# Chunk attention and gated feed-forward on one core: a new order of the first loads, more transposes by DMA, and other transfer times in the planner

## The chip, the core and the metric

The kernel runs on one core of a Trainium2 chip. A core has TensorE (PE, with its weight loads PEld), VectorE (DVE), ScalarE (ACT), GpSimd (POOL), SyncE (SP), which computes nothing and issues transfers here, and 16 DMA engines. The metric is the device time of one execution in microseconds (us), as the median of several runs.

## The reference

Queries, keys and values come as 8 batches x 8 heads x 576 positions x 64. Attention stays inside chunks of 64 positions. Its result, as 4608 tokens x 512, goes through a feed-forward network with four weight matrices.

```python
scores = scale * np.matmul(q_c, k_c.transpose(0, 1, 2, 4, 3))      # per batch, head, chunk: 64 x 64
attn = np.exp(scores - np.max(scores, axis=-1, keepdims=True))
attn = attn / (np.sum(attn, axis=-1, keepdims=True) + 1e-09)
x = np.matmul(attn, v_c)                                           # as 4608 tokens x 512
a = x @ w1                                                         # 512 x 1024
b = x @ w2                                                         # 512 x 1024
out = (a * b @ w3) @ w_out                                         # 1024 x 1024, 1024 x 512
```

## The kernel before, in words

**The work.** All inputs are float32 in memory; the loads, issued on POOL's queue, cast them to bf16 on the way. The tokens are cut into 36 *groups* of 128 (two chunks, all 8 heads), and into 9 *tiles* of four groups (512 tokens) for the feed-forward part. w3 and w_out are multiplied once into one matrix `w3o_sb` (`add_w3o`: w3's 8 row blocks are transposed by PE at L391, copied, and multiplied with `wo_sb` at L402), so that a tile needs only a, b and one output product.

**One group** (`add_group`) goes through these steps:

1. Its q and k land in one buffer `raw` (of 6), 128 tokens x (q, k) x 512.
2. They are transposed. For the groups where `TURN_QK` is false, PE does it with 8 matmuls against the identity matrix (L279, `p_tr` in PSUM), and DVE or ACT copies k out (`kT`) and q out in two halves (`qd`, block-diagonal). Where it is true, SP issues one DMA transpose of the whole buffer (L283, `kqT<-raw`), k is used from where it lands, and only q is copied, in two halves (`qd<-kqT`). Before the change the first such group is 16.
3. PE makes the scores with 8 small matmuls (L307, `p_sc`). DVE and ACT do the softmax (L315 to L334), which ends in `an`.
4. The weights `an` are transposed: by 4 matmuls of PE (L339, `p_at`) and a copy, or, where `TURN_A` is true, by one DMA transpose on SP (L289, `at<-an`). Before the change the first such group is 26.
5. PE multiplies with v (L350, `p_av`, v from `vds`, 3 buffers of a whole batch), and the result is copied to `xt`.

**One tile** (`add_tile`) takes 8 steps of 4 matmuls for a and 4 for b (L432, `ffn<-xt,w_sb`), a copy of a by ACT (`a_sb`), the product a*b by DVE (L441, `abT`), and then four outputs of 8 matmuls each (L457, `ffn<-w3o_sb,abT`), which ACT or DVE copies to `o_sb` and SP sends to memory (L466). These matmuls share four PSUM buffers, `ffn`.

**The order of the work** is made at build time by a small planner (class `Plan`). Each operation is listed with the engines it may run on, a cost, a key (its due time), what it comes after, and the buffers that it takes and that its users hold. `Plan.run` plays a clock: whenever an engine is free it takes the ready operation with the smallest key, and POOL takes its loads strictly in the order of their listing. DMAs of POOL and SP are played as two queues of at most 8 transfers, which share the DMA engines evenly; `flown` is the time up to which the transfers have been played. The resulting order is then written out. On the chip only this order is left: every engine executes its list in order and waits by semaphores, so what the planner thinks of a duration changes only the order in which instructions stand and the engine, DVE or ACT, on which a copy stands.

**The loads.** `LOADS` (L17) lists the first loads on POOL: `("qk", g)` is q and k of group g (two transfers of 256 KB in memory, or four halves where the group spans two batches), `("w3", i, i+1)` one row block of w3 (512 KB), `("wo", ..)` half of w_out (1 MB), `("v", b)` the values of a batch (two transfers), `("w12", ..)` quarter columns of w1 and w2 (four transfers of 256 KB), and `("ident",)` is no load: it makes the identity matrix on POOL, which every transpose by PE needs. After the list, q and k follow group by group, with v between them. A load needs a free buffer: `raw` is free when the group's transposes are done, by PE or by DMA. A ninth load in flight waits for the oldest to land.

Of the kernel before, what the change touches and what calls it, by code (L numbers as in the profile page):

```python
# [13 lines left out]

LOADS = [("wo", 0, 4), ("w3", 0, 1), ("ident",), ("qk", 0), ("qk", 1), ("wo", 4, 8), ("w3", 1, 2), ("qk", 2),  # L17
# [3 lines left out]
TILES = [4] * 9  # L21

TURN_QK = [g >= 16 for g in range(36)]
TURN_A = [g >= 26 for g in range(36)]


class Op:
# [12 lines left out]
class Plan:  # L40
# [33 lines left out]
    def run(self):  # L74
        free = {e: 0.0 for e in ("PE", "ACT", "DVE", "POOL", "SP")}
        free["POOL"] = free["SP"] = 1.2
        todo = {e: [o for o in self.ops if e in o.engines] for e in free}

        rings, flown = {"POOL": [], "SP": []}, 0.0
        left, now, order, ends = len(self.ops), 0.0, [], [1.2]  # L80

        def heads(t):
            return [r[0] for r in rings.values() if r and r[0][0] <= t]

        while left or any(rings.values()):

            while flown < now:
                h = heads(flown)
                step = min([now - flown] + [x[1] * len(h) for x in h])
                step = min([step] + [r[0][0] - flown for r in rings.values() if r and r[0][0] > flown])  # L90
                flown = now if step >= now - flown else flown + step
                for x in h:
                    x[1] -= step / len(h)
                for r in rings.values():
                    if r and r[0] in h and r[0][1] < 1e-6:
                        o = r.pop(0)[2]
                        o.end = flown + o.lag
                        ends.append(o.end)
            for eng in free:
                if free[eng] > now or len(rings.get(eng, ())) >= self.RING:  # L100
                    continue
                if eng == "POOL":
                    pick = [o for o in todo[eng][:1] if self.ready(o, now)]
                else:
                    pick = [o for o in todo[eng] if self.ready(o, now)]
                if not pick:
                    continue
                o = min(pick, key=lambda o: o.key)
                for e in o.engines:
                    todo[e].remove(o)  # L110
                o.start, o.engine = now, eng
                cost = o.cost[o.engines.index(eng)] if isinstance(o.cost, tuple) else o.cost
                if o.issue:
                    free[eng] = now + o.issue
                    rings[eng].append([free[eng], cost, o])
                else:
                    free[eng] = now + cost
                    o.end = now + cost + o.lag
                    ends.append(o.end)
                for n in o.takes:  # L120
                    self.taken[n].append(o)
                order.append(o)
                ends.append(free[eng])
                left -= 1
            ends = [t for t in ends if t > now]
            h = heads(now)
            after = ends + [flown + x[1] * len(h) for x in h]
            assert after or not left, "the plan is stuck"
            now = max(min(after, default=now), now + 1e-6)
        return order  # L130
# [3 lines left out]
def kernel(  # L134
# [51 lines left out]
    ident = consts.tile([P, P], bf)  # L186
# [8 lines left out]
    vds = [wpool.tile([P, NM, NCH, 2 * D], bf, tag=f"vd{i}", name=f"vd{i}") for i in range(BUFS["vd"])]  # L195
    halves = [slice(0, C), slice(C, P)]

    plan = Plan(BUFS, ("qd", "kT", "kqT", "sd", "e", "an", "at"))

    def copy(eng, o, i):  # L200
        if eng == "ACT":
            nc.scalar.copy(o, i)  # L202
        else:
# [4 lines left out]
    zero_v = [plan.add("DVE", 2.0, (-999, -29, 9)[i], lambda eng, t=t: nc.vector.memset(t[:], 0.0))  # L208
              for i, t in enumerate(vds)]


    def load(cost, issue, emit, **kw):
        return plan.add("POOL", cost, 0, emit, lag=landing, issue=issue, **kw)
# [4 lines left out]
    raws, v_got, w12_got, w3_got, wo_got, wo_cut = {}, {}, {}, {}, [], []  # L218
# [13 lines left out]
    def load_v(b):  # L232
        v_got[b] = []
        for t in range(2):
            def emit(eng, t=t):
                nc.gpsimd.dma_start(vds[b % len(vds)][halves[t], :, :, t * D:(t + 1) * D].rearrange("p m c d -> p (m c) d"),  # L236
                                    v[b, NM * t:NM * (t + 1)].rearrange("h (c p) d -> p (h c) d", p=C))
            v_got[b].append(load(2.2, 1.17, emit, takes=() if t else ("vd",), after=(zero_v[b % len(vds)],)))

    def load_w12(j0, j1):  # L240
        for dst, w in ((w1_sb, moe_w1), (w2_sb, moe_w2)):
# [25 lines left out]
    def add_group(g, kt, ks, ka, kv):  # L267
# [3 lines left out]

        turned = TURN_QK[g]

# [81 lines left out]

        got = raws[g]["ops"]
        if turned:
            tr = kc = plan.add("SP", 2.0, kt, qk_turn, after=got, takes=("kqT",), uses=[(got[0], "raw")], lag=2.5, issue=1.3)
            held, cost = [(tr, "kqT")], (0.35, 0.6)
        else:  # L360
            tr = plan.add("PE", 0.46, kt, t_emit, after=got + [made_ident], takes=("p_tr",), uses=[(got[0], "raw")], lag=0.2)
            held, cost = [(tr, "p_tr")], (0.43, 0.66)
            kc = plan.add(("DVE", "ACT"), cost, kt, k_copy, after=(tr,), takes=("kT",), uses=held)
# [3 lines left out]
                     lag=0.2)  # L367
# [3 lines left out]
        sm = plan.add("DVE", 1.1, ks, sum_emit, after=(ex,), lag=0.05)  # L371
        an = plan.add("DVE", 0.7, ks, norm_emit, after=(sm,), takes=("an",), uses=[(ex, "e")])
        if TURN_A[g]:
            ac = plan.add("SP", 1.0, ka, at_turn, after=(an,), takes=("at",), uses=[(an, "an")], lag=2.5, issue=1.3)
        else:
            at = plan.add("PE", 0.23, ka, at_emit, after=(an,), takes=("p_at",), uses=[(an, "an")], lag=0.2)
            ac = plan.add(("DVE", "ACT"), (0.43, 0.66), ka, at_copy, after=(at,), takes=("at",), uses=[(at, "p_at")])
        av = plan.add("PE", 0.24, kv, av_emit, after=[ac] + [o for b, _ in bc for o in v_got[b]], takes=("p_av",),
                      uses=[(ac, "at")] + [(v_got[b][0], "vd") for b in sorted({b for b, _ in bc})], lag=0.2)
# [96 lines left out]
    made_ident, landing = None, 1.6  # L476
    for what, *args in LOADS:
        if what == "ident":
            made_ident = plan.add("POOL", 0.6, 0, lambda eng: make_identity(nc, ident[:]), lag=0.3)
        else:  # L480
            {"qk": load_qk, "v": load_v, "w12": load_w12, "w3": load_w3, "wo": load_wo}[what](*args)
    landing = 2.5
    for g in range(NG):
        if g not in raws:
            load_qk(g)
        b = (2 * max(g - 3, 0) + 1) // NCH
        if b not in v_got:
            load_v(b)

    for g in range(NG):  # L490
        late = min(5 if g < 26 else 3, g // 2)
        add_group(g, *(3 * g - n + late for n in (30 if TURN_QK[g] else 28, 25, 19, 16)))
    for ko in range(FO):
        add_w3o(ko, 0.5 + ko)
# [2 lines left out]
        add_tile(g0, n, lambda j: 3 * g0 + 0.375 * n * j, lambda tk: 3 * (g0 + n) + 1 + 3 * tk)  # L497
        g0 += n
    for c, emit in sorted(outs, key=lambda x: x[0].key):
        plan.add("SP", 0.8, c.key, emit, after=(c,), uses=[(c, "o_sb")], lag=1.6, issue=0.4)  # L500

    with tc.manual_schedule():
        for o in plan.run():
# [31 lines left out]
```

## Time and profile before

| | |
|---|---|
| median of 3 runs | 257.01 us (256.85 to 257.58) |
| the profiled execution | 257.51 us; its span, from the first to the last instruction, is 255.7 us |
| PE busy | 238.2 us, 93% of the span, 1808 matmuls, granted clock 1.0 |
| DVE, ACT, POOL busy | 177.5, 153.6, 102.2 us |
| DMA moved | 35.70 MB, 150598 packets, of which 139696 under 512 B |
| transposes by PE | L279 (`p_tr`) 128 matmuls, L339 (`p_at`) 104 matmuls |
| transposes by DMA | `kqT<-raw` 20, median 7.0 us from issue to landing; `at<-an` 10, median 2.5 us |

The profile shows one execution. Busy times are sums over instructions of one engine; matmuls are pipelined, so that 512 columns take 379 ns from start to end, but the next one starts 216 ns later. The difference of 1.8 us between the profiled execution and its span lies before the first and behind the last instruction. Times in the text are counted from the start of the span. A wait is written with the engine that waited and what ended the wait.

### The profile page before, as it was taken

Reading aid. Unit: us, or ns where it says so; the run is one execution under the profiler, and the core shown is the slowest. Engines: PE = TensorE matmul, PEld = TensorE weight load, DVE = VectorE, ACT = ScalarE, POOL = GpSimd, SP = SyncE. Lnnn points to the kernel's source line nnn. Section 1 sums busy time; section 2 is a strip of 40 time slices with the busy share of each in tenths; the row PEclk is TensorE's granted clock in tenths of the full one; section 3 lists DMA queues with packets and bytes.
Section 4 is the critical chain, followed back from the end, with each engine's and each line's share of the span. In section 5 each row is a group of like instructions: output and inputs, shape, how many; then the busy total and the mean of one; then the engine's idle time right before and its main releaser. Section 6 shows DMA issues by size and latency. Waiting matters only on the chain.

```text
span 255.7 us, 4814 instructions
## 1 busy us (share of the span) xinstructions
PE 238.2 (93%) x1808; PEld 125.9 (49%) x1808; DVE 177.5 (69%) x338; ACT 153.6 (60%) x268; POOL 102.2 (40%) x128
## 2 busy tenths in 40 slices
PE   0469989899999999999999999999999999999994
PEld 0345655456555555555555555444555444444443
DVE  7569999876989778788887877777768772222310
ACT  2247758668988776676766677756675443433232
POOL 8856887989790964723392272000000000000000
PEclk9999999999999999999999999999999999999999
DMA  5999999999999999999999999985422222111123
GB/s 81 163 195 178 180 163 175 162 164 155 169 175 149 205 152 179 186 195 181 183 181 199 182 143 149 185 175 108 105 92 73 62 65 62 41 74 52 41 82 123
DMA packets 150598, 35.70 MB, mean 140 GB/s; under 512 B 139696, under 2 KB 145072, under 8 KB 150576
## 3 DMA queue, kind: packets, MB, share of 16 engines
q0 software_dynamic: 118688, 19.41, 101.6%
q1 hardware_dynamic: 31888, 16.00, 28.7%
q8 instruction: 14, 0.23, 0.3%
q14 instruction: 8, 0.07, 0.1%
HBM read 38.80 MB, written 9.44 MB: 189 GB/s over the span
## 4 chain that ended last, share of the span: by engine, by line
PE 84%; DMA 8%; POOL 2%; ACT 2%; DVE 2%; issue 2%; ACTq 0%; POOLq 0%
PE ffn L432 48%; PE ffn L457 24%; DMA raw<-in_k_dram 5%; PE p_sc L307 3%; PE p_av L350 3%; DMA w_sb<-in_moe_w_dram 3%; PE p_tr L279 2%; PE p_at L339 2%; PE ffn L402 2%; ACT w3t L202 1%; POOL raw L229 1%; DVE qd L204 0%; POOL vd L236 0%; ACT kT L202 0%; DVE ss L327 0%
## 5 line engine op out<-in xcount | busy, mean ns | idle before, releaser
L432 PE MATMUL ffn<-xt,w_sb 128*128 128x512 bf16 x576 | 133.8, 379 | 0.0
L432 PEld LDWEIGHTS <-w_sb 128*128 128x128 bf16 x576 | 54.5, 98 | 60.9
L441 DVE TENSOR_TENSOR abT<-a_sb,ffn 128x512 bf16<-128x512 f32 x72 | 48.4, 673 | 33.1 <-PE ffn L432 31.5
L457 PE MATMUL ffn<-w3o_sb,abT 128*128 128x512 bf16 (+1 forms) x296 | 67.6, 374 | 0.0
L202 ACT COPY a_sb<-ffn 128x512 f32<-128x512 f32 x72 | 41.9, 582 | 27.2 <-PE ffn L432 26.8
L229 POOL DMA_DIRECT2D raw<-in_q_dram x40 | 34.5, 865 | 38.9 <-DMA kqT<-raw 32.4
L457 PEld LDWEIGHTS <-abT 128*128 128x128 bf16 x296 | 27.8, 98 | 29.2
L202 ACT COPY o_sb<-ffn 128x512 f32<-128x512 f32 (+1 forms) x32 | 18.3, 572 | 39.1 <-PE ffn L457 39.1
L327 DVE TENSOR_REDUCE ss<-e 128x8 f32<-128x512 bf16 x36 | 24.6, 682 | 17.3 <-ACT e L323 17.1
L229 POOL DMA_DIRECT2D raw<-in_k_dram x40 | 34.5, 869 | 4.4 <-DMA vd<-in_v_dram 3.1
L315 DVE TENSOR_REDUCE nm<-p_sc 128x8 f32<-128x512 f32 x36 | 24.5, 681 | 3.8 <-PE p_sc L307 3.7
L319 DVE TENSOR_TENSOR sd<-p_sc,nm 128x512 f32<-128x512 f32 x36 | 24.7, 685 | 0.4
L334 DVE TENSOR_TENSOR an<-e,rs 128x512 bf16<-128x512 bf16 x36 | 24.6, 684 | 0.0
L323 ACT ACTIVATE e<-sd 128x512 bf16<-128x512 f32 x36 | 22.7, 631 | 1.6 <-DVE sd L319 1.0
L202 ACT CAST xt<-p_av 128x512 bf16<-128x512 f32 x31 | 18.1, 585 | 8.6 <-PE p_av L350 8.4
L202 ACT COPY qd<-kqT 64x512 bf16<-64x512 bf16 x33 | 20.3, 616 | 0.3
L236 POOL DMA_DIRECT2D vd<-in_v_dram x16 | 18.6, 1176 | 1.9 <-DVE sd L319 1.1
L402 PE MATMUL ffn<-wo_sb,w3t 128*128 128x512 bf16 x64 | 16.7, 396 | 0.8 <-ACT w3t L202 0.7
L350 PEld LDWEIGHTS <-vd 128*128 128x128 bf16 x288 | 13.1, 98 | 8.3 <-issue 1.2
L307 PEld LDWEIGHTS <-qd 128*128 128x128 bf16 x288 | 12.3, 99 | 7.7 <-ACT qd L202 3.0
L350 PE MATMUL p_av<-at,vd 128*128 128x64 bf16 x288 | 14.3, 193 | 0.6 <-DVE xt L204 0.4
L202 ACT COPY qd<-p_tr 64x512 bf16<-64x512 bf16 x22 | 12.8, 580 | 2.0 <-DVE qd L204 1.6
(35 smaller groups left out, 154.4 us busy)
## 6 DMA issues: line engine op xcount, KB each, us to landing
out_dram<-o_sb SPq DMA_DIRECT2D x35, 256.0 KB, 2.3
vd<-in_v_dram POOLq DMA_DIRECT2D x16, 288.0 KB, 7.6
raw<-in_q_dram POOLq DMA_DIRECT2D x32, 128.0 KB, 6.9
raw<-in_k_dram POOLq DMA_DIRECT2D x32, 128.0 KB, 6.7
w_sb<-in_moe_w_dram POOLq DMA_DIRECT2D x8, 256.0 KB, 8.2
w_sb<-in_moe_w_dram POOLq DMA_DIRECT2D x16, 128.0 KB, 6.4
wo_sb<-in_moe_w_out_dram POOLq DMA_DIRECT2D x2, 512.0 KB, 7.3
raw<-in_q_dram POOLq DMA_DIRECT2D x8, 64.0 KB, 7.7
```

What stands on the lines that cost most here:

```text
L202: nc.scalar.copy(o, i)
L229: nc.gpsimd.dma_start(box["t"][r, w], src[b, :, c * C:(c + n) * C, :].rearrange("h p d -> p h d"))
L315: nc.vector.tensor_reduce(nm[:, :, 0], flat(box["sc"]), axis=AX.X, op=ALU.max)
L319: nc.vector.tensor_sub(sd[:], flat(box["sc"]), box["nm"].to_broadcast([P, 8, C]))
L323: nc.scalar.activation(e[:], box["sd"][:], ACT.Exp, scale=scale)
L327: nc.vector.reduce_sum(ss[:], box["e"][:], axis=AX.X)
L334: nc.vector.tensor_mul(an[:], box["e"][:], box["rs"].to_broadcast([P, 8, C]))
L350: nc.tensor.matmul(t[:, m, cc, :], vds[b % len(vds)][:, m, c, :], box["at"][:, 2 * cc + y, u * C:(u + 1) * C], start=True, stop=True)
L402: nc.tensor.matmul(box["wp"][:], box["t"][:, ki, :], wo_sb[:, ki, :], start=(ki == 0), stop=(ki == FO - 1))
L432: nc.tensor.matmul(t[:, :w], wt[:, ki, j * P:(j + 1) * P], x[:, ki, :], start=(ki == 0), stop=(ki == KO - 1))
L441: nc.vector.tensor_mul(box["abT"][:, j, :w], box["as", j][:, :w], box["b", j][:, :w])
L457: nc.tensor.matmul(t[:, :x1 - x0], box["abT"][:, ki, tk * P:(tk + 1) * P], w3o_sb[:, ki, x0:x1], start=(ki == 0), stop=(ki == FO - 1))
```

## The change

The diff has three kinds of edits:

- the order of the first loads (`LOADS`): q and k of groups 0 and 1 go first, w3's first block before w_out's first half, the identity matrix sixth, v of batch 0 and w1, w2 earlier, and the last blocks of w3 later;
- the groups from which DMA transposes take the place of PE's: q and k from group 12 in place of 16, the weights from group 24 in place of 26. `LATE` is a name for a 5 that stood in the code; for groups 24 and 25 the due times now go by 3, as for all groups with turned weights;
- what the planner takes for transfers: 2.0 in place of 2.2 for half of a batch's v, 1.75 for 2.0 and 0.88 for 1.0 for the two transposes, 0.7 for 0.8 for an output, and no transfer is played before 3.4.

The line numbers of the changed kernel are larger by one from L27 on.

```diff
-LOADS = [("wo", 0, 4), ("w3", 0, 1), ("ident",), ("qk", 0), ("qk", 1), ("wo", 4, 8), ("w3", 1, 2), ("qk", 2),
-         ("w3", 2, 3), ("w3", 3, 4), ("qk", 3), ("w3", 4, 5), ("w3", 5, 6), ("qk", 4), ("qk", 5), ("w3", 6, 7),
-         ("w12", 0, 2), ("v", 0), ("w3", 7, 8), ("qk", 6), ("qk", 7), ("w12", 2, 4), ("qk", 8), ("w12", 4, 6),
-         ("v", 1), ("w12", 6, 8), ("qk", 9), ("qk", 10)]
+LOADS = [("qk", 0), ("qk", 1), ("w3", 0, 1), ("wo", 0, 4), ("w3", 1, 2), ("ident",), ("qk", 2), ("wo", 4, 8),
+         ("w3", 2, 3), ("w3", 3, 4), ("w3", 4, 5), ("qk", 3), ("v", 0), ("w3", 5, 6), ("qk", 4), ("w12", 0, 2),
+         ("w12", 2, 4), ("qk", 5), ("w12", 4, 6), ("qk", 6), ("qk", 7), ("w3", 6, 7), ("w12", 6, 8), ("qk", 8),
+         ("w3", 7, 8), ("qk", 9), ("v", 1), ("qk", 10)]
-TURN_QK = [g >= 16 for g in range(36)]
-TURN_A = [g >= 26 for g in range(36)]
+TURN_QK = [g >= 12 for g in range(36)]
+TURN_A = [g >= 24 for g in range(36)]
+LATE = 5
...
-        rings, flown = {"POOL": [], "SP": []}, 0.0
+        rings, flown = {"POOL": [], "SP": []}, 3.4
...
-            v_got[b].append(load(2.2, 1.17, emit, ...
+            v_got[b].append(load(2.0, 1.17, emit, ...
...
-            tr = kc = plan.add("SP", 2.0, kt, qk_turn, ... lag=2.5, issue=1.3)
+            tr = kc = plan.add("SP", 1.75, kt, qk_turn, ... lag=2.5, issue=1.3)
...
-            ac = plan.add("SP", 1.0, ka, at_turn, ... lag=2.5, issue=1.3)
+            ac = plan.add("SP", 0.88, ka, at_turn, ... lag=2.5, issue=1.3)
...
-        late = min(5 if g < 26 else 3, g // 2)
+        late = min(LATE if not TURN_A[g] else 3, g // 2)
...
-        plan.add("SP", 0.8, c.key, emit, after=(c,), uses=[(c, "o_sb")], lag=1.6, issue=0.4)
+        plan.add("SP", 0.7, c.key, emit, after=(c,), uses=[(c, "o_sb")], lag=1.6, issue=0.4)
```

More of the change, by code (lines that the diff above doesn't have):

```diff
@@ L237, in emit @@
                                     v[b, NM * t:NM * (t + 1)].rearrange("h (c p) d -> p (h c) d", p=C))
-            v_got[b].append(load(2.2, 1.17, emit, takes=() if t else ("vd",), after=(zero_v[b % len(vds)],)))
+            v_got[b].append(load(2.0, 1.17, emit, takes=() if t else ("vd",), after=(zero_v[b % len(vds)],)))
     def load_w12(j0, j1):
@@ L357, in add_group @@
         if turned:
-            tr = kc = plan.add("SP", 2.0, kt, qk_turn, after=got, takes=("kqT",), uses=[(got[0], "raw")], lag=2.5, issue=1.3)
+            tr = kc = plan.add("SP", 1.75, kt, qk_turn, after=got, takes=("kqT",), uses=[(got[0], "raw")], lag=2.5, issue=1.3)
             held, cost = [(tr, "kqT")], (0.35, 0.6)
@@ L373, in add_group @@
         if TURN_A[g]:
-            ac = plan.add("SP", 1.0, ka, at_turn, after=(an,), takes=("at",), uses=[(an, "an")], lag=2.5, issue=1.3)
+            ac = plan.add("SP", 0.88, ka, at_turn, after=(an,), takes=("at",), uses=[(an, "an")], lag=2.5, issue=1.3)
         else:
```

## The prediction

> **What bounds the kernel now.** I read PE's busy time by stretch first, then the waits of the first 52 us, then the transposes by DMA. The stretches (columns: stretch and its length; busy time and count of each engine; clock, DMA share, GB/s):
>
> ```profile
> 0.00:52.00 52.00, 37.86 (x367) 23.11 (x368) 42.12 (x79) 28.30 (x45) 40.57 (x59) 1.00 1.68 163
> 52.00:252.00 200.00, 200.00 (x1442) 102.71 (x1440) 135.35 (x260) 124.96 (x222) 61.60 (x70) 1.00 1.23 134
> ```
>
> The first engine is PE. From 52 to 252 us it is busy all 200 us, and I found consecutive matmuls starting at their bare spacing there (216 ns for 512 columns, 56 for 128, 29 for 64). So the time is 14.1 us of PE idle ahead of 52, PE's work, and about 3.7 us behind the last matmul. Shortening DVE, ACT or DMA alone gives nothing there. The waits up to 52 us (who waited for what: total, times, longest):
>
> ```profile
> PE ffn L391 <- DMA w_sb<-in_moe_w_dram: 8.9, 1, 8.9
> ...
> PE p_sc L307 <- ACT qd L202: 1.8, 1, 1.8
> ...
> PE p_tr L279 <- DMA raw<-in_k_dram: 1.6, 3, 0.8
> ```
>
> PE's first work waits 8.9 of the 14.1 us for w3's first block; 5.3 us are later short waits. PE's and POOL's timelines of the start:
>
> ```profile
> 8.88 1.03 PE L391 MATMUL ffn<-ident,w_sb 128*128 128x128 bf16 x8 [8.88 <-DMA w_sb<-in_moe_w_dram]
> ...
> 17.65 0.61 PE L391 MATMUL ffn<-ident,w_sb 128*128 128x128 bf16 x8
> ```
> ```profile
> 1.25 0.89 POOL L260 DMA_DIRECT2D wo_sb<-in_moe_w_out_dram  x1 [0.80 <-POOLq L519]
> 2.13 0.56 POOL L253 DMA_DIRECT2D w_sb<-in_moe_w_dram  x1
> 2.66 0.24 POOL masks.py:197 MEMSET ident<- 128x128 bf16 x1
> ```
>
> The same eight matmuls take 1.03 us at 8.88 and 0.61 at 17.65: PE begins at half speed. Last, `kqT` between 60 and 100 us, then after 168 us, when all loads have landed, and who waits for it:
>
> ```profile
> DMA to landing us min/median/max: 5.5/7.9/10.2
> ```
> ```profile
> DMA to landing us min/median/max: 3.1/3.1/3.1
> ```
> ```profile
> POOL raw L229 <- DMA kqT<-raw: 32.4, 9, 6.9
> ```
>
> A turn beside loads lands after 8 us, alone after 3.1. Only POOL waits for it: the first turn is issued at 73.6 and its scores start at 94.8, a lead of 21 us.
>
> **The change, part by part.**
>
> *1. PE work removed.* Groups 12 to 15 lose 8 transposes each, groups 24 and 25 lose 4: 32 + 8 = 40 matmuls (the new order has 96 and 96 for 128 and 104). In the chain of waits 8 cost 0.45 us on PE:
>
> ```profile
> 57.68 0.45 PE p_tr L279 x8
> ```
>
> 4 x 0.45 + 2 x 0.22 = **2.25 us** off PE. All of it lies in the stretch where PE never waits, so all of it counts, if nothing else comes late. The copies of k and of the weights go too (at 0.59 us on ACT); ACT and DVE are not the bound, so this counts 0.
>
> *2. PE's first work.* It is now the transpose of group 0, which needs q, k and the identity. POOL starts at 1.25 and issues, by its rows, 4 x 0.87 (q, k of two groups), 0.55 (w3), 0.80 (w_out), 0.55 (w3), then makes the identity (0.24 and 0.29, with small gaps): 7.3 us. k of group 0 lands earlier: the old first load (1 MB, 2.5 us of the queue) lands at 7.6, and successive q and k loads land 0.86 apart, so q ends at 7.6 - 2.5 + 0.9 = 6.0 and k at 6.8. First work at 7.35 against 8.88: **-1.5 us**. Bounds: 0 if the first landing comes as late as the old one plus k (8.5), -1.6 if only the identity rules.
>
> *3. Later waits in the first 60 us.* In the old landings I read these spacings while the queue is full: q or k 0.86, w3 block 1.25, half of w_out 2.5, half of a v 1.95, w1/w2 quarter 0.65. With these, and each engine's instructions strictly in the new order at the durations of their rows, I walked both orders. The old walk gives 7.6 us of waits behind PE's first work (the trace 5.3), the new one 6.7 to 7.2. The largest new ones: 1.1 at 8.3 (q copies of group 0), 1.2 at 11.5 (w_out lands at 12.1), 0.9 at 17.2 (q copies of group 2), 0.6 at 27.3. I take **-0.3**, bounds -0.9 and +1.5 (w3's last blocks now come later, and a walk that is wrong by 2.3 on the old order may be so here). The slow start (24 transposes and 4 wide matmuls, 2.2 us lost in the old trace) stays within these waits.
>
> *4. Four more turns of q and k, two of weights, on DMA.* The price is lead. PE's order has 57.1 us of matmuls ahead of group 12's scores; with 18.5 us of waits, drains and slow start in the old trace (94.8 less 76.4 us of matmuls ahead), less the 1.8 of parts 2 and 3, they come at 73.8. Its loads: 26 x 0.86 + 4 x 1.95 + 8 x 1.25 + 5.0 + 16 x 0.65 = 55.6, from 5.1 on, lands at 60.7, or 62 with the 1.6 us by which POOL's stops delayed the old list. Lead 12 us against the old 21. The turn takes 7.9 of it, the q copies 1: 3 us to spare, 0.6 at the worst landing of 10.2. In the walk the leads of groups 12 to 17 are 11 to 16 us, the shortest at group 17, and back near 20 from group 20 on. They are short since `raw` is now held for 8 us more by four more groups (POOL's wait above starts earlier).
>
> What a turn takes of the DMA engines decides whether leads recover. Steady part: from 111.5 to 123.8 us two halves of v, four q/k loads, two outputs and two turns land; 12.2 - 3.9 - 3.4 - 2 x 0.66 = 3.6, **1.8 per turn**. Bounds: 1.1 (in a stretch around 90 us its packets all pass in that time) and 2.6 (from 78.7 to 82.1 only one load lands beside one turn: 3.4 - 0.86). At 1.8 a group needs 1.72 (q, k) + 0.87 (its v) + 0.66 + 1.8 = 5.05 us of DMA, and PE gives it 24 x 0.216 + 3 x 0.23 = 5.87. So DMA gains 0.8 us per group. At 2.6 it is 5.85: no recovery. Weights turned in groups 24 and 25 add a shorter turn (about 1.1, by the lengths alone, 2.5 for 3.1) while loads still run.
>
> The q copies stand on ACT and DVE in order: a late turn holds the copies of a and the products behind it, and PE, with four `ffn` buffers, 4 x 0.86 us later. SP has the turns between outputs; a turn behind an output waits for its copy, up to 1 us here. My walk gives 0.3 to 3 us of new waits; I take **+1.0**; bounds 0 and +6.
>
> A rule that speaks against this part: the Trainium skill, "DMA: Bandwidth & Descriptors", section "Issuing engines are not separate DMA queues", says that transfers issued from SP, ACT and GpSimd all run on the same 16 DMA engines and interleave. By that rule the turns come out of the loads' time, and the trace agrees (8 us beside loads, 3.1 alone). The same page, "Latency and other measured facts", has 261 GB/s for transposes; an estimate from it is 1.0 us for 256 KB, and by it this part would add nothing; the trace's 1.8 decides.
>
> *5. Planner's costs, due times.* They act only through the order, which is in 2 to 4. The end (four outputs, 5 us of matmuls, a copy, a transfer) is unchanged.
>
> **Sum.** -2.25 - 1.5 - 0.3 + 1.0 = -3.05 us. From the profiled 257.51 that is 254.5; the median of the runs is 0.5 lower, so 257.0 - 3.05 = **254.0 us**.
>
> **Rivals.**
>
> *A, the early lead is lost:* PE starts earlier but only waits longer for w_out and w3; part 2 and 3 cancel. For: three of PE's new early waits are of that kind. Against: the walk. Then -2.25 + 0 to 1: **255.2**.
>
> *B, turns a little late:* +3 instead of +1.0 in part 4 at groups 12 to 17: about **256.5**, within 0.3%.
>
> *C, slower:* turns beside loads take 2.6 and more of the DMA engines, as at 78.7 us. From there leads don't recover: ten groups (12 to 21) each come 0.8 us later than at 1.8, 8 us, less 2 to spare, so +6 in part 4: -4.05 + 6 = +2, **259**. It decides from 2.6 per turn, or from landings over 11 us at groups 12 to 17. For: two such slow episodes in the old trace (78.7, and 151 to 161 us, landing 9.0). Against: six regular turns from 95 to 126 land in 6.3 to 8.0 us. This is what the skill's shared engines would do at their worst.
>
> *D, nothing of the kind:* the matmuls removed were covered by something else. PE's 200 of 200 us speak against it; I give it no chance of its own.
>
> **Chances.** Forecast 0.52, A 0.18, B 0.10, C 0.20. 0.3% (0.8 us) is about what a measurement of this kernel can tell from no change. Faster 0.70 (forecast and A), same 0.10 (B), slower 0.20 (C). The range runs from 252.6 (part 3 at its best, part 4 at 0.3: -4.4) to 257.6, which leaves out most of C and little else.
>
> **What would show it.** PE matmuls 1768; PE's first work near 7.3 us; PE idle ahead of 52 us near 12.3; from 60 us on PE idle of about 1 us in all, around the scores of groups 12 to 17 (72 to 100 us) or outputs behind them; `kqT` landing near 8 us while loads run. Wrong if PE's idle behind 60 us is over 3 us with ACT or DVE waiting for `kqT`, if landings are over 11 us, or if PE's idle in the first 52 us stays at 14.

## The result, and the profile after

The changed kernel takes **260.92 us** (median of 4 runs, 259.65 to 261.09) against 257.14 for the kernel before (four runs here): ratio 1.0135, 95% interval 1.0099 to 1.0171. It is slower; the prediction said 254.0. The profiled execution took 260.77 us (before: 257.51), with a span of 258.9 (255.7).

PE's busy time in the two stretches of the prediction (stretch and its length; busy time and count of PE, PEld, DVE, ACT, POOL; clock, DMA share, GB/s):

```profile
0.00:52.00 52.00, 37.59 (x334) 23.13 (x341) 40.58 (x72) 25.64 (x40) 39.32 (x58) 1.00 1.59 160
52.00:252.00 200.00, 194.57 (x1385) 99.45 (x1409) 144.62 (x283) 114.98 (x203) 62.91 (x71) 1.00 1.38 139
```

Before 52 us PE works no longer than before (37.59 for 37.86), though it starts earlier; and its 200 of 200 us behind 52 are gone. Part of that is no idle time: 32 of the 1768 matmuls have no record in this trace. So I use another sum, which missing records don't touch: from PE's first matmul to its last, less the bare work of all the program's matmuls (count by spacing). **PE lost** by it 9.4 us before and 16.2 us after; cut at 62 us, the loss ahead of the cut is 9.1 us before and 11.7 after, and behind it 0.2 and 4.4 (each to about 0.2). The waits that are new or have changed (who waited for what: total, times, longest):

```profile
POOL raw L230 <- DMA vd<-in_v_dram: 30.5, 9, 5.6
...
ACT qd L203 <- DMA kqT<-raw: 11.5, 8, 3.4
...
PE p_tr L280 <- POOL ident masks.py:199: 7.4, 1, 7.4
...
DVE qd L205 <- DMA kqT<-raw: 5.6, 4, 2.3
...
POOL raw L230 <- DMA kqT<-raw: 4.0, 2, 2.9
...
PE p_av L351 <- DMA at<-an: 3.0, 2, 2.5
PE ffn L403 <- ACT w3t L203: 2.9, 5, 1.1
PE p_sc L308 <- DVE qd L205: 2.8, 2, 2.1
```

PE starts at 7.4, as forecast. But ACT and DVE now wait for turned q and k, which they never did before, and PE for turned weights; POOL's wait for `kqT`, 32.4 us in the kernel before, has shrunk to 4.0; its waits for earlier loads to land have grown (for v alone from 7.2 to 30.5 us). So what holds the loads back is no longer a free `raw` but the transfers themselves. `kqT` from 60 to 100 us, then behind 168 us:

```profile
DMA to landing us min/median/max: 8.6/9.1/10.3
```
```profile
DMA to landing us min/median/max: 3.3/9.9/11.0
```

Behind 168 us a turn took 3.1 us in the kernel before; now it takes 9.9, so loads still run there. The DMA row of the page (40 slices, tenths of busy time), after and then before:

```profile
DMA  8999999999999999999999999999954322111123
```
```profile
DMA  5999999999999999999999999985422222111123
```

The DMA engines are full for about 25 us longer: the last load lands at 190.2 us, at 165.6 before. The chain of waits of the changed kernel shows what that does (start, length, what):

```profile
177.94 0.59 ACT o_sb L203
178.55 0.64 ACT e L324
...
180.91 0.43 DVE an L335
181.33 7.73 DMA at<-an
189.07 0.05 issue
189.11 0.41 PE p_av L351 x8
```

A turn of weights takes 7.73 us beside loads, and PE stands still for the end of it: 2.6 us lost at 189.1, 0.7 at 194.3 in the same way (waits of 2.46 and 0.50 us; the rest is the end of the last matmul before them, 379 ns in place of 216). Another 0.8 us goes at 130.2, where PE waits for DVE's subtraction, 5 us after DVE and ACT had stood 1.3 and 2.3 us for a late `kqT`.

### The profile page after: what moved, and what is told of

Read it like the earlier page. It is cut to its first block, busy times and chain, and to the rows that moved or that the text cites. A ratio compares the mean times of both kernels' runs of the same rounds, so it can differ in the third digit from the quotient of the medians.

```text
span 258.9 us, 4717 instructions
## 1 busy us (share of the span) xinstructions
PE 235.5 (91%) x1736; PEld 124.6 (48%) x1768; DVE 185.2 (72%) x354; ACT 142.4 (55%) x246; POOL 102.2 (39%) x128
## 4 chain that ended last, share of the span: by engine, by line
PE 69%; DMA 17%; POOL 7%; issue 2%; DVE 1%; ACT 1%; SPq 0%; ACTq 0%; DVEq 0%; POOLq 0%
PE ffn L433 40%; PE ffn L458 22%; DMA raw<-in_k_dram 5%; DMA w_sb<-in_moe_w_dram 4%; DMA at<-an 4%; POOL raw L230 4%; DMA wo_sb<-in_moe_w_out_dram 4%; PE p_av L351 3%; PE p_sc L308 2%; POOL w_sb L245 2%; PE p_at L340 1%; PE p_tr L280 1%; SPq L284 0%; POOL vd L237 0%; DVE an L335 0%
## 5 line engine op out<-in xcount | busy, mean ns | idle before, releaser
L433 PEld LDWEIGHTS <-w_sb 128*128 128x128 bf16 x576 | 53.8, 98 | 58.1
L458 PE MATMUL ffn<-w3o_sb,abT 128*128 128x512 bf16 (+1 forms) x287 | 66.3, 373 | 0.4
L203 ACT COPY o_sb<-ffn 128x512 f32<-128x512 f32 (+1 forms) x27 | 15.4, 570 | 29.3 <-PE ffn L458 29.3
L203 ACT COPY qd<-kqT 64x512 bf16<-64x512 bf16 x32 | 19.7, 615 | 11.8 <-DMA kqT<-raw 11.5
L203 ACT CAST xt<-p_av 128x512 bf16<-128x512 f32 x29 | 17.0, 586 | 9.2 <-PE p_av L351 9.2
L280 PE MATMUL p_tr<-ident,raw 128*128 128x128 bf16 x96 | 8.6, 241 | 8.9 <-POOL ident masks.py:199 7.4
## 6 DMA issues: line engine op xcount, KB each, us to landing
out_dram<-o_sb SPq DMA_DIRECT2D x35, 256.0 KB, 5.8
vd<-in_v_dram POOLq DMA_DIRECT2D x16, 288.0 KB, 13.9
raw<-in_q_dram POOLq DMA_DIRECT2D x32, 128.0 KB, 10.3
w_sb<-in_moe_w_dram POOLq DMA_DIRECT2D x8, 256.0 KB, 9.3
```

The lines of the kernel that those rows point to most:

```text
L433: nc.tensor.matmul(t[:, :w], wt[:, ki, j * P:(j + 1) * P], x[:, ki, :], start=(ki == 0), stop=(ki == KO - 1))
L458: nc.tensor.matmul(t[:, :x1 - x0], box["abT"][:, ki, tk * P:(tk + 1) * P], w3o_sb[:, ki, x0:x1], start=(ki == 0), stop=(ki == FO - 1))
```

## The experiments

Theory 1: the six extra turns overfill the DMA engines and come late whatever the plan says. Theory 2: the plan's smaller transfer times are at fault. Theory 3: the new list of loads is. Each ratio is to runs of the kernel before taken alongside, whose medians were 257.2 to 257.5 us.

### The parts one by one

*The list alone* (the new `LOADS` in the kernel before).

> The kernel before with the new list of loads alone. Theory 1 (the six extra turns fill the DMA engines, and what they carry comes late): the list is not at fault; PE starts 1.5 us earlier and what its early waits cost in the changed kernel (1.8 us) may or may not come with it, so 255.6 to 257.4 us, no PE wait over 0.5 us behind 62 us, last load landed at about 165 us. Theory 3 (the list of loads is the cause): it loses at least the 1.8 us in the first 62 us and more behind it, 258 us or more. Theory 2 (the plan's smaller transfer costs are the cause): as theory 1.

Measured: 262.25 us, ratio 1.0192 (1.0164 to 1.0220). Theory 3's side, and more than the whole loss. PE lost 15.4 us, 6.0 more than in the kernel before and all of it ahead of 60 us. The longest new waits are at 10.9 us, where w3's first block is late, and at 58 us:

```profile
PE ffn L391 <- DMA w_sb<-in_moe_w_dram: 2.9, 2, 2.6
PE p_at L339 <- DVE an L334: 2.4, 2, 2.1
```

*The turns alone.*

```diff
-TURN_QK = [g >= 16 for g in range(36)]
-TURN_A = [g >= 26 for g in range(36)]
+TURN_QK = [g >= 12 for g in range(36)]
+TURN_A = [g >= 24 for g in range(36)]
...
-        late = min(5 if g < 26 else 3, g // 2)
+        late = min(5 if not TURN_A[g] else 3, g // 2)
```

> The kernel before with the turns of groups 12 to 15 and 24, 25 moved to DMA alone (and the due times that go with group 24). Theory 1: the loads end about 20 us later than in the kernel before (165), turns of weights land beside loads after 7 us, PE gets waits of 3 us or more behind 150 us: about 257.1 - 2.25 + 4.8 = 259.7 us, not under 257.1. Theory 2: with the old costs the plan leaves room, the 2.25 us of PE work are saved: 254.9 us. Theory 3: also 254.9.

Measured: 256.28 us, ratio **0.9955** (0.9932 to 0.9979): faster. Theory 1 falls in this form. Half of it is there: the loads end at 187.6 us, turns of q and k take a median of 9.0 us and up to 11.9. But hardly anybody waits; behind 62 us all waits for turned tiles except POOL's are

```profile
ACT qd L202 <- DMA kqT<-raw: 0.4, 1, 0.4
```

The 254.9 us of theories 2 and 3 are missed by 1.4: PE lost 1.6 us behind 62 us to short waits, 0.2 in the kernel before.

*The transfer times alone* (2.2 to 2.0, 2.0 to 1.75, 1.0 to 0.88, 0.8 to 0.7, `flown` 0.0 to 3.4).

> The kernel before with the plan's new transfer times alone (2.0, 1.75, 0.88, 0.7 and nothing flown before 3.4 us). Theory 1: they act through the order alone and there are no more turns than before: 257.1 us, within 0.8. Theory 2: the plan counts on transfers that come sooner than DMA gives, so ACT and DVE wait for kqT or at behind 62 us and PE loses some 3 to 5 us: 260 to 262 us.

Measured: 258.65 us, ratio 1.0041 (1.0024 to 1.0059). Between the theories: ACT now waits 6.4 us for `kqT`, but PE loses only 1.0 us more than before, and that ahead of 52 us.

*All but the turns.*

> The changed kernel with the turns back at groups 16 and 26 (new list of loads and new transfer times stay). Theory 1: the late waits are gone, the loads end near 165 us, what is left is the start: 257.1 - 1.5 + 1.8 = 257.4 us, or 255.6 if the early waits of the changed kernel go too. Theory 2 and theory 3: the loss stays, 259 to 263 us.

Measured: 258.33 us, ratio 1.0035 (1.0019 to 1.0052). So list and transfer times together cost 0.8 us where the list alone costs 4.8, and the turns, which gain 1.2 us on the kernel before, cost 2.6 on this one. No part has a price of its own; the parts act on each other, and the plan is where they can. Theory 2b: more turns do harm where the plan is told that a turn is cheaper than it is.

### Which pair does the harm

*The changed kernel with all old transfer times:*

> The changed kernel with the old transfer times in the plan (new list and new turns stay). After the first four runs the turns alone gain 1.2 us, the list alone loses 4.8, the costs alone 1.2, list and costs together 0.8. Theory 2b (the extra turns are harmful only where the plan is told that a transfer is cheaper than it is): the wait of PE for turned weights near 189 us is gone, PE's idle behind 165 us is under 1.5 us, the loads still end near 187 us, and the list's loss stays: 262.2 - 1.2 = 261.0 us. Theory 1 (the turns' transfers are late whatever the plan says): the wait near 189 us stays, 262.2 - 2.25 + 5 = 265 us.

Measured: 261.28 us, ratio 1.0177 (1.0132 to 1.0221), as theory 2b has it: no PE wait for a turned tile, and the whole loss of 16.2 us ahead of 62 us, with the list's wait at 58 us again.

*The changed kernel with the old list:*

> The changed kernel with the old list of loads (new transfer times and new turns stay). Theory 2b: costs and turns together make the late waits, so waits for at or kqT of 3 us or more stay behind 120 us: 258.6 - 2.25 + 4 = 260.4 us. Theory 3 (the new list is the cause, alone or with the turns): 258.6 - 1.2 = 257.4 us, PE's waits behind 120 us under 1.5 us in all.

Measured: 259.61 us, ratio 1.0098 (1.0069 to 1.0126). Nearer to theory 2b (260.4): one PE wait of 2.3 us for turned weights at 187 us, and 17.1 us of ACT's and DVE's waits for `kqT`:

```profile
ACT qd L203 <- DMA kqT<-raw: 10.0, 11, 1.9
...
DVE qd L205 <- DMA kqT<-raw: 7.1, 4, 3.3
...
PE p_av L351 <- DMA at<-an: 2.3, 1, 2.3
```

All eight combinations of list, turns and transfer times are now measured. Behind 62 us PE lost 4.3 us here and 4.4 in the changed kernel, 1.6 with the turns alone, and 0.2 to 0.4 in the five others. So the late loss needs the new transfer times and the turns, not the list.

*The two turn costs alone put back:*

```diff
-            tr = kc = plan.add("SP", 1.75, kt, qk_turn, after=got, takes=("kqT",), uses=[(got[0], "raw")], lag=2.5, issue=1.3)
+            tr = kc = plan.add("SP", 2.0, kt, qk_turn, after=got, takes=("kqT",), uses=[(got[0], "raw")], lag=2.5, issue=1.3)
...
-            ac = plan.add("SP", 0.88, ka, at_turn, after=(an,), takes=("at",), uses=[(an, "an")], lag=2.5, issue=1.3)
+            ac = plan.add("SP", 1.0, ka, at_turn, after=(an,), takes=("at",), uses=[(an, "an")], lag=2.5, issue=1.3)
```

> The changed kernel with the plan's two old turn costs alone (2.0 for q and k, 1.0 for weights; 2.0 for v, 0.7 for an output and the 3.4 us stay). Theory 2b, in the form that the turns' costs are the ones that count: the wait near 189 us is gone or under 1 us, 258.3 - 2.25 + 1.0 = 257.1 us. Theory 1, or theory 2b with the cost of v and the 3.4 us as the ones that count: the late waits stay, 260 to 261 us.

Measured: **256.24 us**, ratio 0.9962 (0.9944 to 0.9981). Two numbers, which nothing on the chip reads, are worth 4.7 us. Behind 62 us PE lost only 0.3 us (4.4 in the changed kernel); ahead of it 11.6, as the changed kernel did (11.7). From 165 to 190 us, the changed kernel and then this one:

```profile
165.00:190.00 25.00, 22.38 (x164) 11.06 (x166) 18.72 (x40) 13.04 (x24) 3.77 (x4) 1.00 1.73 158
```
```profile
165.00:190.00 25.00, 24.84 (x182) 12.55 (x184) 18.41 (x36) 16.85 (x30) 4.95 (x5) 1.00 1.72 171
```

DMA is as full (1.73 and 1.72; the loads end even later, at 192.6 us), the turns take as long (7.8 us for the one of weights issued at 183.3), and PE is busy. What differs is how long after its landing a turned tile is first needed: for the fourth to seventh turn of weights 0.9, 0, 0, 0 us in the changed kernel, 2.9, 3.6, 0.7, 0.9 here.

*The changed kernel with less on the DMA engines*, in its own order:

```diff
             def emit(eng, t=t):
+                if t and b > 2:
+                    return
```

> The changed kernel in its own order, but the second half of v is not loaded for batches 3 to 7 (those halves hold what an earlier batch left, so the output differs there): five transfers of 1.95 us less on the DMA engines between about 60 and 190 us, nothing moved. Theory 1 and 2b (what is late is the transfers, the DMA engines being full to 190 us): the loads end about 10 us earlier, the waits of PE near 130, 189 and 194 us go, 260.9 - 0.8 - 3.3 = 256.8 us. Rival (the waits come from the order on ACT and DVE, not from transfers): within 0.8 us of 260.9.

Measured: 256.39 us, ratio 0.9966 (0.9942 to 0.9991). The same order is good when the transfers come in time: PE never waits for a turned tile, ACT and DVE wait 3.4 and 2.2 us (11.5 and 5.6 in the changed kernel), and behind 62 us PE lost 0.4 us. The loads end at 167.3 us, 23 us earlier and not the 10 expected; why so much earlier was not taken apart. The rival falls: the order on ACT and DVE is not slow by itself.

```profile
ACT qd L203 <- DMA kqT<-raw: 3.4, 4, 1.4
...
DVE qd L205 <- DMA kqT<-raw: 2.2, 2, 1.5
```

### More and less of the turn cost

*1.6 and 0.8:*

> The changed kernel with the plan's turn costs lower still: 1.6 for q and k, 0.8 for weights (changed: 1.75 and 0.88, 260.9 us; the run with 2.0 and 1.0: 256.2 us). Theory 2b (below the true 2.0 every order comes out too tight): waits of PE, ACT and DVE for kqT and at grow over those of the changed kernel, 261.5 to 264 us. Rival (any new order falls somewhere within 3 us by luck, the cost has no side): as likely below 259 as above, and no more waits for kqT and at than before.

Measured: 263.84 us, ratio 1.0238 (1.0176 to 1.0299). ACT's and DVE's waits for turned tiles grew as expected (11.5 and 5.6 us in the changed kernel); PE's own for turned weights did not (3.0), but behind 62 us PE lost 7.3 us in all (4.4):

```profile
ACT qd L203 <- DMA kqT<-raw: 25.3, 15, 4.7
DVE qd L205 <- DMA kqT<-raw: 8.9, 5, 4.0
...
PE p_av L351 <- DMA at<-an: 2.9, 2, 2.3
```

*1.87 and 0.94:*

> The changed kernel with turn costs of 1.87 and 0.94, half way. Theory 2b: between the two, 257 to 259 us, waits for at and kqT on PE of 1 to 3 us behind 120 us. Rival (luck): outside of that.

Measured: 257.79 us, ratio 1.0013 (0.9985 to 1.0041). The time is where it was expected; the waits are not: they are on ACT (6.2 us) and DVE (2.3), and PE, for which 1 to 3 us were expected, has none for a turned tile itself.

*2.25 and 1.12:*

> The changed kernel with turn costs of 2.25 and 1.12, over the true 2.0. Theory 2b: no wait of PE for kqT or at over 0.3 us; but the plan, which now counts on transfers that take longer than they do, keeps PE back elsewhere (its order waits for copies and products late in the span): 257 to 260 us. Rival (a dearer turn only ever adds safety): 256.2 us or less.

Measured: 259.21 us, ratio 1.0059 (1.0035 to 1.0083). But for POOL (12.1 us) nobody waits for a turned tile; behind 62 us PE lost 3.1 us, and waits there for copies:

```profile
PE ffn L433 <- ACT xt L203: 1.3, 2, 0.7
PE p_sc L308 <- ACT o_sb L203: 1.1, 1, 1.1
```

With 1.6, 1.75, 1.87, 2.0, 2.25 the times are 263.8, 260.9, 257.8, 256.2, 259.2. The time falls to 2.0 and rises behind it, with waits for turned tiles on the one side and for copies on the other. That speaks for a curve and against luck, for this list and these other times.

*1.87 and 0.94, with the turns of groups 12 to 15, 24 and 25, on the kernel before* (old list, other old times):

> The kernel before with the turns of groups 12 to 15 and 24, 25 moved to DMA, and turn costs of 1.87 and 0.94 (old list, the other old costs). Theory 2b: the other old costs (v 2.2, an output 0.8) keep the plan's end of the loads where it is, so there are no late waits, and the 1.0 us of order waits that ate part of the 2.25 in the run with the old costs may go: 255 to 256.3 us, the best of all. Rival (a turn cost under 2.0 is always too low): waits for at or kqT behind 120 us, 257 us or more.

Measured: **255.74 us**, ratio 0.9928 (0.9902 to 0.9955), the lowest of the study; PE lost 9.6 us and waits for no turned tile behind 62 us. The rival falls: under 2.0 isn't always too low. Why it does no harm here is argued and not shown: the other times of this plan (v 2.2 where 1.95 was read, an output 0.8 where 0.66) leave room. Nor is it shown to be better than the turns alone at 2.0 and 1.0 (256.28 us), as the intervals overlap.

### Where the early start went

PE, ACT and DVE at the start of the changed kernel:

```profile
10.47 0.61 PE L308 MATMUL p_sc<-kT,qd 128*128 128x64 bf16 x8 [2.10 <-DVE qd L205]
...
13.89 1.89 PE L403 MATMUL ffn<-wo_sb,w3t 128*128 128x512 bf16 x4 [1.10 <-ACT w3t L203]
```
```profile
7.73 1.98 DVE L209 MEMSET vd<- 128x2304 uint32 x1 [0.43 <-issue]
9.62 0.79 DVE L205 COPY qd<-p_tr 64x512 bf16<-64x512 bf16 x2
```

The third memset of a v buffer ends at 9.7 us. The first q copy came at 12.4 in the kernel before, 2.7 us behind it; now it waits for it. Behind that stands w_out's first half, which lands at 13.2 us (13.9 in the kernel of 256.24 us). To take the memset away alone, the kernel of 256.24 us was emitted in its own order with that one instruction moved:

```diff
+        if g == 1:
+            plan.q1 = q1
...
-        for o in plan.run():
+        order = plan.run()
+        order.remove(zero_v[2])
+        order.insert(order.index(plan.q1) + 1, zero_v[2])
+        for o in order:
```

> The run with turn costs 2.0 and 1.0 (256.2 us) in its own order, but for one instruction: the third memset of a v buffer stands behind the q copies of group 1 on VectorE, not ahead of those of group 0. Theory 4 (two waits in series, the memset and then w_out's landing): PE's wait of 2.1 us near 10.4 us shrinks by about 1.2 us, the wait of 1.2 us for w_out near 14 us grows by as much, the time stays within 0.5 us of 256.2. Rival (the memset alone takes the start's gain): 255.0 us.

Measured: 256.32 us, ratio 0.9955 (0.9931 to 0.9978): no gain, as theory 4 has it. The first wait shrank by 0.5 us (not 1.2: the q copies now wait for ACT's k copy), the second grew by 0.3 (1.19 us in the kernel of 256.24 us), in a profiled execution of 257.25 us, above the median:

```profile
9.94 0.61 PE L308 MATMUL p_sc<-kT,qd 128*128 128x64 bf16 x8 [1.57 <-DVE qd L205]
...
13.75 1.86 PE L405 MATMUL ffn<-wo_sb,w3t 128*128 128x512 bf16 x4 [1.50 <-DMA wo_sb<-in_moe_w_out_dram]
```

Then both: the memset planned behind the q copies of group 1 (`zero_v[2].after.append(q1)`), and the list begun with

```diff
-LOADS = [("qk", 0), ("qk", 1), ("w3", 0, 1), ("wo", 0, 4), ("w3", 1, 2), ("ident",), ("qk", 2), ("wo", 4, 8),
+LOADS = [("qk", 0), ("w3", 0, 1), ("ident",), ("wo", 0, 4), ("qk", 1), ("w3", 1, 2), ("qk", 2), ("wo", 4, 8),
```

> The run with turn costs 2.0 and 1.0 (256.2 us), the third memset behind the q copies of group 1, and the list of loads with w3's first block, the identity and w_out's first half ahead of q and k of group 1. Theory 4: w_out lands about 1.7 us earlier, at 12 us, PE's first work comes at about 6.8 us, and both waits shrink: 254.0 to 255.4 us. Rival (the early part is bound by the sum of what must land, whatever the order): within 0.6 us of 256.2.

Measured: 255.89 us, ratio 0.9938 (0.9914 to 0.9962): where the rival had it. PE's first work came at 7.24 us, not at 6.8, but w_out landed at 11.1, and the waits did shrink,

```profile
11.13 1.87 PE L405 MATMUL ffn<-wo_sb,w3t 128*128 128x512 bf16 x4 [0.68 <-DMA wo_sb<-in_moe_w_out_dram]
```

and PE lost 11.0 us for 11.9 in the run with turn costs 2.0. But the profiled execution, 255.27 us, is the fastest of its six, and the ratio's interval overlaps that run's (0.9944 to 0.9981), so a gain isn't shown.

The same two edits (the list of this run is called e14 in what follows) on the kernel of 255.74 us:

> The best run so far (old costs but 1.87 and 0.94 for the turns, 255.7 us) with the third memset behind the q copies of group 1 and the list of e14. Theory 4 and 2b together: no late waits for turned tiles over 1 us on PE, the start's gain kept, 254.0 to 255.2 us. Rival (the list of loads costs more than the start brings, as alone): 256.5 us or more.

Measured: 256.78 us, ratio 0.9982 (0.9960 to 1.0004). On the rival's side. Theory 2b's part held (no PE wait for a turned tile), theory 4's did not. In its profiled execution (258.49 us, above the median) w_out comes only at 12.7 us, and PE lost 13.4 us, nearly all of it ahead of 62. Whether the list or that execution is to blame was not taken apart.

## Why the prediction was wrong

Point by point, in the profile of the changed kernel:

1. *PE work removed, -2.25:* right. The order has 1768 matmuls, their bare work is 2.24 us less.
2. *PE's first work, -1.5:* right, and for the reason given: k had landed at 6.5 us, and PE waited for the identity. 7.36 for 8.88 us.
3. *Later waits in the first 60 us, -0.3 (bounds -0.9 and +1.5):* wrong, and outside its bounds: about **+2.5** (1.8 ahead of 52 us, 0.7 at 60). The walk saw most of the early waits, but too small. It had 1.1 us for the wait before group 0's scores, and it was 2.1, the memset among it; w_out's first half at 12.1, and it landed at 13.2; 0.6 near 27, where 0.9 came at 29.8; and nothing at 44.8, where PE waited 1.1 for a late k. The forecast counted the early start as gained and the waits as a small correction; here the waits grew by more than the start gained. This is what rival A described, at more than its price.
4. *Turns by DMA, +1.0 (bounds 0 and +6):* right in sign and within its bounds, but **+4.1** (0.8 at 130 us, 3.3 at 189 and 194). Two terms were mis-sized. First the turn: from 70 to 185 us 64.3 load transfers (by packets, 0.85 us for 1024, the rate of loads alone), 18.0 outputs at 0.66 and 24.8 turns (one of weights counted as half) share 115 us, which leaves **1.95 us per turn**, not 1.8; the same sum gives 1.93 to 2.04 in the eleven other runs that have these turns and all loads, and 1.97 in the kernel before (70 to 165 us). I had read it from 12 us, too short a stretch. Second the turns of weights, which I priced as two and short. Once they run, a group needs 1.72 + 0.87 + 0.66 + 2.0 + 1.0 (half a turn, an estimate) = 6.25 us of DMA. PE gives it less than the 5.87 of the prediction, as the transposes of weights are gone too: 24 x 0.216 + 2 x 0.23 = 5.64, the spacing of the last groups' products with v in the kernel before (191.33 and 196.97). So behind group 24 leads shrink as long as loads run. In the kernel before that state lasted 6 us (first turn of weights at 159.3, last load at 165.6), in the changed one 40 (149.9 to 190.2), and six turns of weights fell into it at 6.8 to 8.6 us each.
5. *Planner's costs, "They act only through the order, which is in 2 to 4":* **this is the step that failed**, together with the size of part 3. The costs do act through the order only, but part 5 put them at nothing, and they are worth 4.7 us: with 2.0 and 1.0 in the plan, and with nothing else changed, the same turns, list and loads take 256.24 us in place of 260.92, 0.4% less than the kernel before, and the loss behind 62 us falls from 4.4 to 0.3. Why the walk of that same order didn't show this is argued and not shown, as it was not done again at 1.95: it took 1.8 per turn, next to the 1.75 that the order was made for, and so found the plan in time with itself.

So of the 6.9 us between forecast and measurement the planner's turn costs make 4.7. The 2.2 that are left (256.24 for 254.0) come for the most part from part 3, 2.8 more than forecast, less the 0.9 by which part 4 comes out under its +1.0 once the costs are right: the kernel with the old turn costs lost as much ahead of 62 us as the changed one.

-2.25 - 1.5 + 2.5 + 4.1 = +2.85, and 0.2 more at the end; the spans of the profiled executions (258.85 and 255.73 us) differ by 3.1. The signs named for a wrong forecast came true too: PE idle behind 60 us over 3, with ACT and DVE waiting for `kqT`. What the walk said of the leads of groups 12 to 17 (11 to 16 us, the shortest at group 17) held: from issue to scores they are 10.3 to 15.8 us, 10.3 at group 17. That they are "back near 20 from group 20 on" did not: 18.4, 17.7, and then 13.4 us at group 22, behind whose late turn the 0.8 us at 130 went.

Of the rivals, C had the sign and nearly the time (259), but not its mechanism, so that its time came near is luck: no turn took 2.6 us over a longer stretch, and it named groups 12 to 21, whereas most of the late loss stands at groups 29 and 30. The 2.6 was read from 78.7 to 82.1 us; from 80.0 to 80.75 hardly a packet of any queue passes there (70 in all, where soon after some 205 pass in a third of that time), so the stretch held a gap and no slower turn. Its "leads don't recover" did come true, by turned weights beside loads. B's own sum, with +3 in part 4, gives 256.0 and not 256.5.

The Trainium skill's rule that I weighed against the change ("DMA: Bandwidth & Descriptors", "Issuing engines are not separate DMA queues") held: the turns came out of the loads' time, which ended 25 us later. By the 261 GB/s that the same page of the Trainium skill, "Latency and other measured facts", has for transposes, a turn would take an estimated 1.0 us. The trace has 1.4 us from the first to the last packet of a turn alone, and 1.95 us of DMA for one beside loads.

What stays open: why the new list costs 4.8 us under the old transfer times and about nothing under v 2.0, an output 0.7 and 3.4 us of delay (which of the three does it was not tried), and how much of the early start is to be had at all.

## What to carry to other kernels

Where a program orders its instructions by assumed durations, a duration that is too small makes no instruction slower but takes the slack out of every in-order queue. Measure the assumed transfer in the state in which it will run, next to the traffic it will run next to, and check an order with measured durations, not with those that it was made from. Before moving work to a shared resource, sum its need per iteration in each stage, the last ones too: here, by the sum above, it passed what PE gave it only where two kinds of turns and the loads overlapped. And when the start is brought forward, look at what was hidden behind the old start, on every engine.

## What the runs showed of the hardware

A turn of q and k (256 KB from SBUF to SBUF, 1024 packets on SP's queue) takes 1.4 us from its first to its last packet when it is alone, and 3.1 us from issue to landing (kernel before, behind 168 us). Beside POOL's loads the packets of the two queues pass one for one in the trace's packet records: some 205 of each in half a microsecond, where loads alone pass some 600. So while a turn's packets pass, the loads move at about a third of their speed. In the changed kernel a turn's packets then take 2.7 to 4.0 us, 3.0 in the median; as the loads go on meanwhile, it costs them less, the 1.95 us of the sum above. But more than half of the 9 us to landing lies ahead of all this: beside loads a turn's first packet moves 5.2 us after the issue (median of 23), alone 1.2. What it waits for there the runs don't show.
